# Scores and slot reads in the h banks, two tiled groups a batch, and later x loads

## The chip, the cores and the metric

The kernel runs on one core of a Trainium2 chip. The metric is the time of one execution on the device, in microseconds (us), as the median of several runs; profiles are one execution each. "Span" is the time from the first to the last instruction of the profiled execution. Every run has a state: fast, or slow when it is more than 1.5% above the fastest run of the same kernel. Ratios below use fast runs alone; a median is over all runs of a kernel.

## The reference, cut to what matters

```python
def _attn_ref(x, state):              # x (8, 8, 512, 64), state (8, 8, 32, 64)
    scores = scale * np.matmul(x, state.transpose(0, 1, 3, 2))
    a = softmax(scores)               # each token over the 32 slots
    xread = np.matmul(a, state)
    scores2 = scale * np.matmul(state, x.transpose(0, 1, 3, 2))
    a2 = softmax(scores2)             # each slot over the 512 tokens
    sread = np.matmul(a2, x)
    return np.concatenate([xread, sread], axis=2)

def _moe_ref(x, w_in, w_out, s, b):   # x (4352, 512), w_in (512, 2048)
    r = np.maximum(x @ w_in, 0.0)
    return (s * (r * r) + b) @ w_out
```

The softmaxes are abbreviated here. Both read the same scores, once along the slots and once along the tokens.

## The kernel before

The kernel first builds M = state x w_in for a batch, so that `a @ M` gives the hidden layer directly. It loops over batches s = 1 to 7. While it computes the products of batch s it prepares batch s+1: scores T, their exponential E, its transpose ET, the normalized shares, four chunks of M, and the slot reads V. I call one turn of this loop a **stage**. A stage has 16 "h pairs", f = 0 to 15, and the products of the second layer are spread between them as 112 products of 256 columns each. Each h pair goes through relu on ACT (`r`) and a square on DVE (`g`). The second layer is made of seven block products instead of eight, the **fast products**: they read sums of token blocks (`s`) and differences of weight blocks (`wd`), add up in oA, oB and oC, and DVE keeps the partial results `qa`, `qb` and `u`. For a batch below NDT the denominators of the shares come from products (D). From NDT on DVE makes them from ET, and a transfer brings the shares back as a4; I call this the **transposed softmax**.

Four buffers and queues matter to the argument. The first is how the PSUM banks are shared out: two "att" tiles for the preparation, two "h" banks for the hidden layer, and two for the output.

```python
    psA = ctx.enter_context(tc.tile_pool(name="psA", bufs=2, space=bass.MemoryType.PSUM))
    psH = ctx.enter_context(tc.tile_pool(name="psH", bufs=2, space=bass.MemoryType.PSUM))
    psO = ctx.enter_context(tc.tile_pool(name="psO", bufs=2, space=bass.MemoryType.PSUM))
```

The second is the SP queue. Every transposing transfer is issued there, in program order: xT (x transposed, which T multiplies), ET, a4 (the shares transposed back), the slot reads (srT) and stT (the state of batches 3 to 7 transposed).

```python
    def att_xT_dma(b):
        xT = new_xT(b)
        nc.sync.dma_start_transpose(
            out=xT.rearrange("p h k t -> p (h k) t"),
            in_=xn[b].rearrange("p h c d -> p (h c d)"),
        )
    ...
    def att_a4_dma(b):
        a = A[b]
        a["a4"] = apool.tile([P, NG, S], FP16, name=f"a4_{b}", tag="a4")
        nc.sync.dma_start_transpose(
            out=a["a4"].rearrange("p g (c t) -> p (g c) t", c=SCH),
            in_=a["aT"].rearrange("t j p -> t (j p)"),
        )
```

The third is the POOL queue, which issues the x loads and the output stores. The fourth is DVE, which makes the shares, the squares of relu, the sums of token blocks (`s`) that the fast products read, and the outputs (`osb`).

```python
            nc.vector.reduce_sum(den, ET_s, axis=mybir.AxisListType.X)
            with nc.allow_low_precision("shares are fp16"):
                nc.vector.reciprocal(inv, den)
            nc.vector.tensor_mul(...)            # aT = ET x inv, cut
```

The schedule of a stage says after which pair f a piece stands in the program. It sets the order in each queue; it does not set a time. This is the list of before for s of 2 and more, with its last lines cut:

```python
            if s + 3 < B:
                at(13 if s == 2 else 2, lambda: load_x(s + 3))
            if s == 2:
                at(0, stT_dma)
            if nb < B:
                at(3, lambda: att_T(nb, [0, 1]))
                at(3, lambda: att_M(nb, 0, "act"))
                at(4, lambda: att_ET(nb))
                if s in (2, 3):
                    at(4, lambda: att_xT_dma(nb + 1))
                if s >= 3 and s + 3 < B:
                    at(13, lambda: att_xT_dma(s + 3))
                if nb < NDT:
                    at(5, lambda: att_D(nb, [0, 1]))
                else:
                    at(8, lambda: att_shares(nb))
                    at(9, lambda: att_a4_dma(nb))
                at(7, lambda: att_M(nb, 1, "act"))
                at(7, lambda: att_M(nb, 2, "act"))
```

The softmax here doesn't subtract the row's maximum and nothing guards it: scores larger than these inputs give would overflow.

## Time and profile before

| | before |
|---|---|
| time, median of the first 3 runs | 211.18 us (211.03 to 213.14) |
| span of the profile | 208.0 us |
| last product of PE starts | 204.09 us |
| start of stage s=1, its length | 26.99, 25.27 us |
| stages s=2 to s=6 | 23.24, 21.27, 21.27, 21.28, 21.27 us |
| from the start of s=7 to the end | 47.41 us |

Stage lengths run from the first h product of a batch to the first one of the next. The prediction below shows the views on which it rests. The list of issues on the SP queue has the columns start, time on the queue, engine, line, operation, tiles and count.

### The profile page before, as it was taken

What the parts mean: (1) busy time and instruction counts of PE and PEld (TensorE: products, weight loads), DVE (VectorE), ACT (ScalarE), POOL (GpSimd) and SP (SyncE); (2) the same over time, 40 slices, a digit from 0 to 9 for tenths busy, and PEclk for the clock granted to TensorE, in tenths of its full rate; (3) what the DMA queues carried; (4) which work ended last, traced back from release to release, by engine and by line L of the source; (5) the groups of instructions that cost most, each with busy time, mean ns of one, the idle gap of its engine ahead of it and who ended that gap; (6) DMA issues with size and microseconds to landing.
All of it is one profiled execution on the core that took longest, in us unless ns stands there. A gap on an engine that the chain in (4) does not pass through costs nothing.

```text
span 208.0 us, 4757 instructions
## 1 busy us (share of the span) xinstructions
PE 199.5 (96%) x1947; PEld 129.4 (62%) x1947; DVE 162.1 (78%) x282; ACT 125.3 (60%) x218; POOL 37.6 (18%) x64
## 2 busy tenths in 40 slices
PE   7888999999899999999999999999999999999992
PEld 2433343445566676667666766676667777788882
DVE  1587825978769796899779977998799877895862
ACT  3678865698489557765776477656774544533100
POOL 5970001501110330123011201120111012100210
PEclk9999999999999999999999999999999999999999
DMA  5999996999947299979833915231324111110143
GB/s 183 225 202 206 207 191 104 179 181 174 266 52 153 72 194 123 124 163 185 127 103 67 196 52 102 54 107 54 101 29 132 50 54 50 54 50 0 54 145 111
DMA packets 45946, 25.35 MB, mean 122 GB/s; under 512 B 30884, under 2 KB 43940, under 8 KB 45924
## 3 DMA queue, kind: packets, MB, share of 16 engines
q0 software_dynamic: 15536, 16.19, 38.8%
q1 hardware_dynamic: 29588, 8.49, 23.8%
q10 hardware_dynamic: 800, 0.36, 0.7%
q8 instruction: 15, 0.25, 0.5%
q14 instruction: 7, 0.06, 0.1%
HBM read 17.33 MB, written 8.91 MB: 126 GB/s over the span
## 4 chain that ended last, share of the span: by engine, by line
PE 82%; DVE 6%; DMA 6%; ACT 4%; issue 1%; POOL 0%; SPq 0%; POOLq 0%
PE h L70 23%; PE oB L70 17%; PE oC L70 12%; PE oA L70 10%; PE o L70 6%; PE Mps L70 4%; DMA wi<-in_moe_w_in_dram 4%; PE h_sr L70 3%; DMA stT_all<-st 2%; ACT r L365 2%; DVE g L371 1%; PE T L70 1%; PE oB_sr L70 1%; PE V L70 1%; DVE M L298 1%; PE oA_sr L70 1%
## 5 line engine op out<-in xcount | busy, mean ns | idle before, releaser
L365 ACT ACTIVATE r<-h 128x512 f16<-128x512 f32 x126 | 74.4, 601 | 52.0 <-PE h L70 51.4
L70 PE MATMUL h<-a,M 128*128 128x512 f16 x256 | 75.0, 379 | 0.9 <-DVE M L298 0.6
L371 DVE TENSOR_TENSOR g<-r 128x1024 f16<-128x1024 f16 x64 | 44.1, 691 | 16.0 <-ACT r L365 15.8
L70 PEld LDWEIGHTS <-s 128*128 128x128 f16 x448 | 42.8, 98 | 19.3 <-issue 3.7
L70 PEld LDWEIGHTS <-g 128*128 128x128 f16 x400 | 38.0, 98 | 18.9 <-issue 2.9
L536 POOL DMA_DIRECT2D out_dram<-osb x27 | 18.2, 675 | 125.5 <-DVE osb L528 120.3
L70 PE MATMUL oB<-wd,s 128*128 128x256 f16 x224 | 32.7, 273 | 0.0
L70 PE MATMUL oA<-wo,g 128*128 128x256 f16 x224 | 31.6, 273 | 0.1
L70 PEld LDWEIGHTS <-M 128*128 128x128 f16 x256 | 24.6, 98 | 10.9 <-DVE M L298 1.6
L301 ACT CAST M<-Mps 128x1024 f16<-128x1024 f32 x27 | 26.8, 1017 | 1.4 <-PE Mps L70 0.8
L70 PE MATMUL oC<-wd,s 128*128 128x256 f16 x112 | 16.5, 273 | 0.0
L70 PE MATMUL o<-wo,g 128*128 128x512 f16 x64 | 16.3, 380 | 0.0
L70 PE MATMUL oB<-wd,g 128*128 128x256 f16 x112 | 15.9, 273 | 0.0
L70 PE MATMUL oC<-wo,s 128*128 128x256 f16 x112 | 15.3, 273 | 0.0
L365 ACT ACTIVATE r_sr<-h_sr 128x256 f16<-128x256 f32 x16 | 6.1, 382 | 8.4 <-PE h_sr L70 8.4
L227 ACT ACTIVATE E<-T 128x512 f16<-128x512 f32 x16 | 9.4, 596 | 1.2 <-PE T L70 1.1
L471 DVE TENSOR_TENSOR s<-s,g 128x1024 f16<-128x1024 f16 x14 | 9.7, 691 | 0.4
L70 PE MATMUL h_sr<-srdT,wi 128*128 128x256 f16 x64 | 9.6, 273 | 0.0
L465 DVE TENSOR_TENSOR s<-g 128x1024 f16<-128x1024 f16 x14 | 9.6, 685 | 0.0
L473 DVE TENSOR_TENSOR s<-g,s 128x1024 f16<-128x1024 f16 x14 | 9.6, 684 | 0.0
L469 DVE TENSOR_TENSOR s<-g,g 128x1024 f16<-128x1024 f16 x14 | 9.6, 683 | 0.0
L528 DVE SCALAR_TENSOR_TENSOR osb<-oC,s_bc,u 128x512 f32<-128x512 f32 x12 | 8.9, 746 | 0.5 <-PE oC L70 0.5
(102 smaller groups left out, 187.4 us busy)
## 6 DMA issues: line engine op xcount, KB each, us to landing
out_dram<-osb POOLq DMA_DIRECT2D x31, 256.0 KB, 2.8
xn<-in_x_dram POOLq DMA_DIRECT2D x7, 512.0 KB, 7.0
wi<-in_moe_w_in_dram POOLq DMA_DIRECT2D x4, 512.0 KB, 9.2
wo<-in_moe_w_out_dram POOLq DMA_DIRECT2D x4, 512.0 KB, 15.9
xf<-in_x_dram SPq DMA_DIRECT2D x2, 512.0 KB, 4.8
out_dram<-osb_sr SPq DMA_DIRECT2D x8, 32.0 KB, 1.6
out_dram<-osb_sr ACTq DMA_DIRECT2D x8, 32.0 KB, 1.7
out_dram<-osb_last SPq DMA_DIRECT2D x2, 128.0 KB, 1.9
```

The costliest lines, as they stand in the source:

```text
L70: return nc.tensor.matmul(out, lhsT, rhs, start=start, stop=stop, tile_position=tp, is_transpose=is_transpose, skip_group_check=True,)
L227: nc.scalar.activation(a["E"][:, g, :].rearrange("p (m t) -> p m t", m=2), T[:, :, 256 * i : 256 * i + 256], AF.Exp, scale=scale, accum_ou ...
L298: nc.vector.tensor_copy(dst[:, 0], two[0])
L301: nc.scalar.copy(dst, ps)
L365: nc.scalar.activation(r16[:, f % 2], hps, AF.Relu)
L371: nc.vector.tensor_mul(gt[:, f % 4 - 1 : f % 4 + 1], r16, r16)
L465: nc.vector.tensor_sub(o, a11, a21)
L469: nc.vector.tensor_add(o, a21, a22)
L471: nc.vector.tensor_sub(o, SQ[b, 1, j], a11)
L473: nc.vector.tensor_sub(o, a12, SQ[b, 2, j])
L528: nc.vector.scalar_tensor_tensor(osb, acc[bank], s_bc, add, ALU.mult, ALU.add)
L536: nc.gpsimd.dma_start(dst[j][:, :, n0 : n0 + NH], osb)
```

## The change

Its intent is to take overhead off PE, which bounds the kernel (it holds 82% of the chain of before): two groups of tiled products instead of three in a batch, scores and slot reads in the h banks so that the att tiles are free for M, and no D products for batch 3. The slot-read scaling goes from DVE to ACT. The x loads move later, and xT of the next batch moves behind a4. The diff, cut to its core:

```diff
-    NDT = 4
+    NDT = 3
...
+        one_bank = b >= NDT
+        if one_bank:
+            Ts = [psH.tile([P, NG, S // 2], FP32, tag="h", name=f"T_{b}_{m}") for m in range(2)]
...
+        if one_bank:
+            for m in range(2):
+                for g in gs:
+                    nc.scalar.activation(
+                        a["E"][:, g, 256 * m : 256 * m + 256],
+                        Ts[m][:, g, :],
+                        AF.Exp,
...
+        if b >= NDT - 1:
+            ps = psH.tile([P, NG, D], FP32, tag="h", name=f"V_{b}")
...
-        for g in range(NG):
-            nc.vector.tensor_scalar(a["sr"][:, g], ps[:, g], a["rq"][:, g : g + 1], None, ALU.mult)
+        with tc.issue_after(G["relu"]):
+            for g in range(NG):
+                nc.scalar.mul(a["sr"][:, g], ps[:, g], a["rq"][:, g : g + 1])
...
+                at(7, stT_dma)                                   # in stage s=1
...
-                at(13 if s == 2 else 2, lambda: load_x(s + 3))
-            if s == 2:
-                at(0, stT_dma)
+                at(13 if s == 2 else 12, lambda: load_x(s + 3))
             if nb < B:
-                at(3, lambda: att_T(nb, [0, 1]))
-                at(3, lambda: att_M(nb, 0, "act"))
+                ahead(4, lambda: att_M(nb, 0, "later"))
+                ahead(4, lambda: att_T(nb, [0, 1]))
+                ahead(4, lambda: att_M(nb, 1, "later"))
                 at(4, lambda: att_ET(nb))
-                if s in (2, 3):
-                    at(4, lambda: att_xT_dma(nb + 1))
-                if s >= 3 and s + 3 < B:
-                    at(13, lambda: att_xT_dma(s + 3))
...
+                at(4, lambda: A[nb]["M", 0]())
+                at(6, lambda: A[nb]["M", 1]())
+                at(8, lambda: att_shares(nb))
+                at(9, lambda: att_a4_dma(nb))
+                if nb + 1 < B:
+                    at(9, lambda: att_xT_dma(nb + 1))
...
+            ahead(10, lambda: att_V(s))
+            if nb < B:
+                ahead(10, lambda: att_M(nb, 2, "later"))
+                ahead(10, lambda: att_M(nb, 3, "later"))
+                at(10, lambda: A[nb]["M", 2]())
+                at(12, lambda: A[nb]["M", 3]())
...
+                if s > 1 and 4 <= f < 13:
+                    for fn in items[f]:
+                        fn()
+                    items[f] = []
```

More of the change, by code (lines that the diff above doesn't have):

```diff
@@ L210, in att_T @@
         a = A[b]
-        n = len(gs)
-        T = att_ps([P, 2, 512], FP32, f"T_{b}_{gs[0]}")
+        one_bank = b >= NDT
+        if one_bank:
+            Ts = [psH.tile([P, NG, S // 2], FP32, tag="h", name=f"T_{b}_{m}") for m in range(2)]
+        else:
+            T = att_ps([P, 2, 512], FP32, f"T_{b}_{gs[0]}")
+            Ts = [T[:, m, 0 : 256 * len(gs)].rearrange("p (g t) -> p g t", t=256) for m in range(2)]
         for q in range(NQ):
@@ L217, in att_T @@
                     mm(
-                        T[32 * q : 32 * q + 32, m, 256 * i : 256 * i + 256],
+                        Ts[m][32 * q : 32 * q + 32, i, :],
                         st_of(b, h, m),
@@ L224, in att_T @@
             a["E"] = apool.tile([P, NG, S], FP16, name=f"E_{b}", tag="E", bufs=3)
-            a["rs"] = apool.tile([P, NG], FP32, name=f"rs_{b}", tag="rs", bufs=4)
+            n = 2 * NG if one_bank else NG
+            a["rs"] = apool.tile([P, n], FP32, name=f"rs_{b}", tag="rs", bufs=4)
+        if one_bank:
[5 more added lines that the diff above has]
+                        AF.Exp,
+                        scale=scale,
+                        accum_out=a["rs"][:, NG * m + g : NG * m + g + 1],
+                    )
+            return
         for i, g in enumerate(gs):
@@ L277, in att_a4_dma, with copy_M @@
         )
+    def copy_M(dst, ps):
+        with tc.issue_after(G["relu"]):
+            nc.scalar.copy(dst, ps)
     def att_M(b, c, how):
@@ L296, in att_M @@
         dst = a["M"][:, :, FC * c : FC * c + FC]
-        if how == "split":
+        if how == "later":
+            a["M", c] = lambda: copy_M(dst, ps)
+        elif how == "split":
             nc.vector.tensor_copy(dst[:, 0], two[0])
@@ L309, in att_ET @@
         a["rq"] = apool.tile([P, NG], FP32, name=f"rq_{b}", tag="rq", bufs=4)
-        nc.vector.reciprocal(a["rq"], a["rs"])
+        rs = a["rs"]
+        if b >= NDT:
+            rs = apool.tile([P, NG], FP32, name=f"rt_{b}", tag="rt")
+            nc.vector.tensor_add(rs, a["rs"][:, 0:NG], a["rs"][:, NG : 2 * NG])
+        nc.vector.reciprocal(a["rq"], rs)
     def att_V(b):
         a = A[b]
-        ps = att_ps([P, NG, D], FP32, f"V_{b}")
+        if b >= NDT - 1:
+            ps = psH.tile([P, NG, D], FP32, tag="h", name=f"V_{b}")
+        else:
+            ps = att_ps([P, NG, D], FP32, f"V_{b}")
         for g in range(NG):
@@ L326, in att_V @@
         a["sr"] = apool.tile([P, NG, D], FP16, name=f"sr_{b}", tag="sr")
-        for g in range(NG):
-            nc.vector.tensor_scalar(a["sr"][:, g], ps[:, g], a["rq"][:, g : g + 1], None, ALU.mult)
+        with tc.issue_after(G["relu"]):
+            for g in range(NG):
+                nc.scalar.mul(a["sr"][:, g], ps[:, g], a["rq"][:, g : g + 1])
     def att_srT_dma(b):
@@ L365, in mm1_close @@
             nc.scalar.activation(r16[:, f % 2], hps, AF.Relu)
+            G["relu"] = nc.cur_bb.bb.instructions[-1]
         if f % 4 == 0:
@@ L756, in at, with ahead @@
                 out.setdefault(f, []).append(fn)
+            def ahead(f, fn):
+                out.setdefault((f, "ahead"), []).append(fn)
             if s == 1:
@@ L780, in pieces @@
             if s + 3 < B:
-                at(13 if s == 2 else 2, lambda: load_x(s + 3))
-            if s == 2:
-                at(0, stT_dma)
+                at(13 if s == 2 else 12, lambda: load_x(s + 3))
             if nb < B:
-                at(3, lambda: att_T(nb, [0, 1]))
-                at(3, lambda: att_M(nb, 0, "act"))
+                ahead(4, lambda: att_M(nb, 0, "later"))
+                ahead(4, lambda: att_T(nb, [0, 1]))
+                ahead(4, lambda: att_M(nb, 1, "later"))
                 at(4, lambda: att_ET(nb))
-                if s in (2, 3):
-                    at(4, lambda: att_xT_dma(nb + 1))
-                if s >= 3 and s + 3 < B:
-                    at(13, lambda: att_xT_dma(s + 3))
-                if nb < NDT:
-                    at(5, lambda: att_D(nb, [0, 1]))
-                else:
-                    at(8, lambda: att_shares(nb))
-                    at(9, lambda: att_a4_dma(nb))
-                at(7, lambda: att_M(nb, 1, "act"))
-                at(7, lambda: att_M(nb, 2, "act"))
+                at(4, lambda: A[nb]["M", 0]())
[4 more added lines that the diff above has]
+                    at(9, lambda: att_xT_dma(nb + 1))
             if s == 2:
@@ L802, in pieces @@
                 at(12, lambda: att_srT_dma(1))
-            at(10, lambda: att_V(s))
+            ahead(10, lambda: att_V(s))
[4 more added lines that the diff above has]
+                at(12, lambda: A[nb]["M", 3]())
             if s == last_b:
@@ L807, in pieces @@
                 at(12, lambda: att_srT_dma(s))
-            if nb < B:
-                at(10, lambda: att_M(nb, 3, "act"))
             if s == last_b:
@@ L832 @@
             for f in range(NKF):
+                for fn in todo_s.get((f, "ahead"), []):
+                    fn()
+                if s > 1 and 4 <= f < 13:
+                    for fn in items[f]:
+                        fn()
+                    items[f] = []
                 mm1_x(s, f)
```

## The prediction

> **What bounds the kernel now.** I read the page first (engine shares, chain of waits), then the stretches view cut at batch boundaries, then the PE, ACT, DVE and SP timelines. The chain:
>
> ```profile
> PE 199.5 (96%) x1947; PEld 129.4 (62%) x1947; DVE 162.1 (78%) x282; ACT 125.3 (60%) x218; POOL 37.6 (18%) x64
> ...
> PE 82%; DVE 6%; DMA 6%; ACT 4%; issue 1%; POOL 0%; SPq 0%; POOLq 0%
> ```
>
> The set-up and batch 0 hold most of the chain's DMA and DVE part; from about 58 us on it is PE. The loop over batches s = 1..7 computes s's products while it prepares batch s+1. I place its stage starts at the 16 h pairs (two 512-column products each):
>
> ```profile
> 52.26:75.50 23.24, 22.42 (x261) 14.89 (x259) 18.66 (x33) 16.06 (x26) 3.50 (x5) 1.00 0.64 136
> 75.50:96.77 21.27, 21.27 (x227) 14.58 (x224) 18.68 (x31) 14.17 (x25) 3.61 (x5) 1.00 1.03 154
> 96.77:118.05 21.28, 21.28 (x227) 14.59 (x225) 18.68 (x31) 14.18 (x25) 3.60 (x5) 1.00 0.65 127
> ```
>
> After the window come its length, then PE, PEld, DVE, ACT and POOL busy. Stages s=3 to s=6 each take 21.27 us with PE full; s=2 takes 23.24. Clock is 1.00, so a gain must take work or gaps off PE. PE's timeline in s=3, start time first:
>
> ```profile
> 84.55 0.59 PE L70 MATMUL h<-a,M 128*128 128x512 f16 x2
> 85.08 0.63 PE L70 MATMUL Mps<-wi,stT_all 64*32 64x512 f16 x16
> 85.64 0.94 PE L70 MATMUL oC<-wd,s 128*128 128x256 f16 x7
> 86.41 0.59 PE L70 MATMUL h<-a,M 128*128 128x512 f16 x2
> 86.84 0.93 PE L70 MATMUL oC<-wd,s 128*128 128x256 f16 x7
> ...
> 88.80 0.59 PE L70 MATMUL h<-a,M 128*128 128x512 f16 x2
> 89.33 0.42 PE L70 MATMUL V<-xn,ET 128*32 128x64 f16 x32
> 89.67 0.41 PE L70 MATMUL Mps<-wi,stT_all 64*32 64x512 f16 x8
> 90.02 0.94 PE L70 MATMUL oB<-wd,g 128*128 128x256 f16 x7
> ```
>
> Starts, not durations, are to be read. An h pair costs 0.43 (86.41 to 86.84), seven 256-column products 0.77. Before a tiled group the pair takes 0.53, so **entry costs 0.10**. Sixteen Mps take 0.56; eight of them cost 0.213 (T, also eightfold parallel, takes 0.23 ahead of Mps in one mode), so 0.43 is work and **exit costs 0.13**. V to Mps changes the mode again, 0.34 for about 0.21 of work. A stage has three groups: T+M0 (after pair 3), M1+M2 (after 7), V+M3 (after 10). Overhead is 3 x 0.23 + 0.13 = 0.82. Check: 112 x 0.109 + 16 x 0.43 + four M x 0.213 + T 0.21 + V 0.21 + 0.82 = 21.2, against 21.27.
>
> Stage s=2's excess of 1.97 us:
>
> ```profile
> 54.67 0.59 PE L70 MATMUL h<-a,M 128*128 128x512 f16 x2
> 55.29 0.94 PE L70 MATMUL oB<-wd,s 128*128 128x256 f16 x7
> 56.06 0.59 PE L70 MATMUL h<-a,M 128*128 128x512 f16 x2
> 57.45 0.43 PE L70 MATMUL T<-xT,stT_all 64*32 64x256 f16 x16 [0.79 <-DMA stT_all<-st]
> ```
>
> T starts 1.39 after its pair instead of 0.53: 0.86 lost to the stT transpose, which the SP timeline shows issued at 52.83 and the transfers view landing 4.6 us later. The oB products start 0.62 after their pair, 0.19 late; the waits view names DVE's token sum. The rest is D of batch 3 (two products, 0.43) and a second V in a group of its own (0.10 + 0.35): 0.86 + 0.19 + 0.43 + 0.45 = 1.93.
>
> [...]
>
> **The change part by part.**
>
> *Two groups instead of three* (M0+T+M1 before pair 4, V+M2+M3 before pair 10), s=2 to s=6: one entry and one exit fewer, 0.23 each.
>
> *h banks.* T takes both. ACT's timeline in s=2, where nothing queues before it:
>
> ```profile
> 57.98 0.60 ACT L227 ACTIVATE E<-T 128x512 f16<-128x512 f32 x1 [0.69 <-PE T L70]
> 58.48 0.19 ACT L227 ACTIVATION_READ_ACCUMULATOR E<-T 128x1 f32 x1
> 58.57 0.59 ACT L227 ACTIVATE E<-T 128x512 f16<-128x512 f32 x1
> ```
>
> T starts at 57.45, M at 57.68, call that t; Exp starts at t+0.30 and the pitch is 0.59. With 256 columns it is 0.59 - 0.21 = 0.38. The first bank's two Exps and the last accumulator read end near t+0.30+0.38+0.48 = 1.16, plus 0.06 to reach PE (an assumption) = 1.22. On PE there now lie M1 0.21, exit 0.13 and seven products 0.77 before pair 4: t+1.11. So a stall of at most 0.11; I count half. The second bank is free at about t+1.9, pair 5 due at 2.3: no wait. V's bank: V finishes about 1.07 after pair 9's start, relu 9 ends at 1.23, [...]and its next user comes at about 3.4: none. Net 0.17 per stage, 5 x 0.17 = **-0.85**.
>
> *ACT* gains four Exp passes for two (4 x 0.38 - 2 x 0.59 = +0.34)[...], off the path. M0's copy (1.02) after relu 4 delays relu 5 by some 0.3, while its bank is not wanted for 1 us.
>
> *Slot reads off DVE:* -0.47 per batch, on DVE alone. For V of batch 0 (DVE at 50.91, in a stretch 99% busy) it lets the sums come 0.4 earlier, which should remove the 0.19 stall: **-0.19**.
>
> *Transposed softmax for batch 3:* D's two products go, **-0.43**; ACT loses 1.02 + 1.06. DVE gains 1.21 + 0.35 + 1.23 and loses the 0.69 multiply and two scaling pairs (0.94): +1.2 on 18.7 in a stage of some 21.5. The shares have about 8 us until their use: hidden.
>
> *stT transpose in stage s=1:* SP is free at 39.5, the state copy on POOL was done at 33.0; it lands near 44. T of batch 3 then waits only for its xT, issued at 46.2, which lands near 52 to 54: **-0.86**.
>
> *Late x loads:* no PE wait names them; 0.
>
> *Order.* Fast products now come before pairs 4 to 12, after from 13, so pairs 12 and 13 adjoin. In s=7 slot products lie between: h12, h_sr, h13. h13 needs h12's bank, whose relu ends 1.23 after h12's start (85.18 + 0.60 against 84.55); h13 is due at 0.87: **+0.4**. In other stages pair 13 needs pair 11's bank, long free.
>
> Sum: -0.85 - 0.19 - 0.43 - 0.86 + 0.4 = -1.93, so 211.18 - 1.93 = 209.25, say **209.2 us**.
>
> **Rivals.** *The lent banks starve PE.* If ACT runs an M copy before the Exps, or relu 3 is late, pair 4 waits another 1.0 per batch: +5, about 214. For: only two h banks, and Tile orders ACT itself. Against: the copies are tied behind relu 4, and ACT idles 0.6 between relus. *The stT wait merely becomes an xT wait.* The earlier transpose shares DMA engines (share above 1.0 in s=1) with the x load on which xT 3 waits. If it slips over 3 us the 0.86 stays: 210.1. Against: T also moves one pair later. *DVE becomes the bound in s=2:* shares delay the squares, relu buffers fill, PE stops; a microsecond at most, about 210.2. For: DVE at 4.93 of 5 us in 85 to 90, where shares run now. Against: PE showed no gap there. *Larger gain:* no bank stall, no tail stall, tiled gaps smaller than thought: about -2.6, 208.6.
>
> **Range and chances.** The gain terms sum to -2.6 with no losses; the likely single failures add 0.5 to 1. Runs before spread by 1% (211.03 to 213.14). So 207.9 to 210.8. Faster by 2% needs 206.96, twice my gain: 0.05. Slower by 2% needs the starved banks: 0.03.
>
> **What will show it.** Right: two tiled groups per stage; stages s=3 to s=6 at 21.05 to 21.15; s=2 near 21.6 with T not waiting on stT; pair 4 no later than 1.22 after M1's start; a 0.4 gap before h13 in s=7. Wrong: PE rows waiting on E or relu each stage, stages above 21.3, or T waiting on xT.

The step that V's bank holds nothing up, and the one that ACT stays off the path, are estimates. In after the two scalings of batch 0 took 0.53 us together (at 50.49), and ACT was busy for 14.61 to 14.65 us in each of the stages s=3 to s=6.

Figures without a row beside them in that text have these in before. Products of 256 columns last 273 ns and start 0.11 us apart. Eight Mps take 0.22 us (43.11 to 43.33) and T 0.23 (57.45 to 57.68), so 0.213 and 0.21 are estimates, half of an h pair's 0.43. A change of "mode" is a change of the tile shape in the rows (128*128, 64*32, 128*32). An ACT pass takes 596 ns for 512 columns (Exp) and 382 for 256 (relu), which differ by the 0.21 that is subtracted for the pitch of the Exps. From the end of an accumulator read on ACT to the product that needs it PE took 0.05 us (21.49 to 21.54), where 0.06 is assumed. The DMA share of s=1 is 1.17.

## More of the kernel before

```profile
81.49 1.26 SPq L308 DMA_TRANSPOSE ET<-E  x1
82.84 3.83 SPq L204 DMA_TRANSPOSE xT<-xn  x1
90.04 1.23 SPq L274 DMA_TRANSPOSE a<-aT  x1
```

This is stage s=3, which starts at 75.50. The xT row is that of batch 5, and it is issued right behind ET of batch 4. Batch 5 needs it for T in stage s=4, which PE starts at 100.88. The transfer therefore has a **lead** of 18 us. Those of batches 6 and 7, issued at 92.94 and 114.21, have 29 us each (T at 122.16 and 143.43).

## The result, and the profile after

| | before | after |
|---|---|---|
| time, median of 4 fast runs | 211.11 us (210.02 to 213.14) | 223.28 us (223.22 to 224.07) |
| span, mean granted clock | 208.0 us, 1.000 | 221.4 us, 0.983 |
| start of s=1, its length | 26.99, 25.27 | 27.16, 25.25 |
| stages s=2, 3, 4, 5, 6 | 23.24, 21.27, 21.27, 21.28, 21.27 | 25.22, 22.90, 28.12, 22.45, 21.55 |
| from s=7 to the end | 47.41 | 48.75 |

The change makes the kernel slower: the ratio is 1.0573, with a 95% interval of 1.049 to 1.0657. A ratio here is always the mean time of one kernel's fast runs over that of the other's of the same rounds, so it is not quite the ratio of the medians quoted. The prediction of 209.2 us in a range of 207.9 to 210.8 missed.

Engine shares, granted clock and chain of waits, from the page of after:

```profile
PE 202.9 (92%) x1945; PEld 130.3 (59%) x1945; DVE 160.2 (72%) x273; ACT 126.9 (57%) x252; POOL 37.6 (17%) x64
...
PEclk9999999999999999999769999999999999999999
...
PE 50%; DMA 27%; DVE 13%; ACT 5%; issue 2%; SPq 1%; POOL 0%; POOLq 0%
DMA xT<-xn 21%; PE h L70 12%; PE oB L70 11%; PE oC L70 7%; DMA xn<-in_x_dram 5%; ACT r L395 3%; PE oA L70 3%; PE o L70 3%; DVE g L402 3%; PE Mps L70 3%; PE warm_ps L70 3%; PE h_sr L70 2%; DVE s L500 1%; PE T L70 1%; PE oB_sr L70 1%
```

PE's part of the chain fell from 82% to 50%. The transposed x, which was on no chain before, holds 21%. Clock is 1.00 but for two slices. The stretches view, cut at the stage starts (columns as in the prediction), shows where:

```profile
52.41:77.63 25.22, 22.27 (x259) 14.68 (x257) 19.63 (x33) 14.99 (x32) 4.18 (x6) 1.00 0.68 133
77.63:100.53 22.90, 21.72 (x227) 14.54 (x224) 18.61 (x31) 14.64 (x31) 3.60 (x5) 1.00 0.67 114
100.53:128.65 28.12, 23.07 (x224) 15.47 (x225) 17.53 (x30) 14.65 (x30) 3.61 (x5) 0.88 0.70 96
151.10:172.65 21.55, 21.43 (x226) 14.62 (x224) 18.18 (x31) 14.61 (x31) 2.71 (x4) 1.00 0.41 96
```

In s=3 to s=6 of before, PE was as busy as the stage was long, and in s=2 it was free for 0.82 us. Now 2.95 of 25.22 us are free in s=2, 1.18 in s=3 and 5.05 in s=4. In s=6, the last row, the gap is small, and still the stage is 0.28 longer than before. PE's timeline names the wait; the bracket at the end is the idle time ahead of the row and what ended it:

```profile
60.45 0.44 PE L70 MATMUL T<-xT,stT_all 64*32 64x256 f16 x16 [1.98 <-DMA xT<-xn]
83.98 0.44 PE L70 MATMUL T<-xT,stT_all 64*32 64x256 f16 x16 [0.72 <-DMA xT<-xn]
110.88 0.65 PE L70 MATMUL T<-xT,stT_all 64*32 64x256 f16 x16 [5.05 <-DMA xT<-xn]
113.36 1.06 PE L70 MATMUL h<-a,M 128*128 128x512 f16 x2
156.65 0.40 PE L70 MATMUL T<-xT,stT_all 64*32 64x256 f16 x16
```

The T of batches 3, 4 and 5 waited 1.98, 0.72 and 5.05 us; that of batch 6 waited another 0.71 (the waits view sums all four to 8.5 us), that of batch 7 none. The row at 113.36 is an h pair that takes 1.06 us where it took 0.59: the clock was lowered in the long wait. The granted clock was 0.62 from 107 to 111 us and 0.53 from 111 to 115, which in these last four loses 0.47 x 4 = 1.9 us; from 115 to 119 it was 1.00. The waits of 1.98 us and less left the clock at 1.00 in this trace, and the one of 5.05 us did not. Waits of other lengths are met below.

Four waits and the slow clock give 8.46 + 1.9 = 10.4 of the 13.4 us that the span grew. The other 3.0 are the subject of the later experiments. (Before had a wait of 0.79 at T itself, for stT; less that, the T waits and the clock account for 9.6.)

Why xT is late can be read from the SP and POOL queues of stage s=3 (start 77.63) and from the median times from issue to landing:

```profile
95.53 1.25 SPq L290 DMA_TRANSPOSE a<-aT  x1
96.87 4.89 SPq L204 DMA_TRANSPOSE xT<-xn  x1
96.99 1.01 POOL L120 DMA_DIRECT2D xn<-in_x_dram  x1
...
xn<-in_x_dram POOLq DMA_DIRECT2D x7, 512.0 KB, 11.7
xT<-xn SPq DMA_TRANSPOSE x6, 9.4
stT_all<-st SPq DMA_TRANSPOSE x1, 14.4
```

The same three transfers took 7.0, 5.8 and 4.6 us before. The xT of batch 5 now stands behind a4 and is issued at 96.87. PE would have started T at 110.88 - 5.05 = 105.83, so the lead is 9.0 us, where it was 18. And the transfer, which was now issued 0.12 us ahead of an x load (96.99 on the POOL queue), took 13.96 us by the chain. 13.96 - 8.96 is the wait of 5.0. The other batches fit the same sum:

| xT of batch | issued | x load issued after it by | xT took | lead to T | T waited |
|---|---|---|---|---|---|
| 4 | 74.00 | 0.78 | 9.94 | 9.26 | 0.72 |
| 5 | 96.87 | 0.12 | 13.96 | 8.96 | 5.05 |
| 6 | 125.52 | 1.08 | 9.53 | 8.86 | 0.71 |
| 7 | 147.97 | no load | not shown | 8.68 | none |

Here the lead is the time from issue to where T would have started without its wait. Moving xT cost it half of its lead, and the late x loads, put into the same part of the stage, made it take longer than what was left.

### The profile page after: what moved, and what is told of

Its sections match the earlier page's. It is cut to its first block, busy times and chain, and to the rows that moved or that the text cites. A ratio compares the mean times of both kernels' runs of the same rounds, so it can differ in the third digit from the quotient of the medians.

```text
span 221.4 us, 4780 instructions
## 1 busy us (share of the span) xinstructions
PE 202.9 (92%) x1945; PEld 130.3 (59%) x1945; DVE 160.2 (72%) x273; ACT 126.9 (57%) x252; POOL 37.6 (17%) x64
## 4 chain that ended last, share of the span: by engine, by line
PE 50%; DMA 27%; DVE 13%; ACT 5%; issue 2%; SPq 1%; POOL 0%; POOLq 0%
DMA xT<-xn 21%; PE h L70 12%; PE oB L70 11%; PE oC L70 7%; DMA xn<-in_x_dram 5%; ACT r L395 3%; PE oA L70 3%; PE o L70 3%; DVE g L402 3%; PE Mps L70 3%; PE warm_ps L70 3%; PE h_sr L70 2%; DVE s L500 1%; PE T L70 1%; PE oB_sr L70 1%
## 5 line engine op out<-in xcount | busy, mean ns | idle before, releaser
L395 ACT ACTIVATE r<-h 128x512 f16<-128x512 f32 x126 | 74.4, 602 | 51.1 <-PE h L70 46.1
L70 PEld LDWEIGHTS <-s 128*128 128x128 f16 x448 | 43.5, 99 | 20.6 <-DVE s L502 3.9
L70 PE MATMUL oB<-wd,s 128*128 128x256 f16 x224 | 33.3, 277 | 0.8 <-DVE s L502 0.4
L70 PEld LDWEIGHTS <-M 128*128 128x128 f16 x256 | 24.6, 98 | 13.3 <-DVE M L320 1.6
L297 ACT CAST M<-Mps 128x1024 f16<-128x1024 f32 x20 | 20.1, 1006 | 0.0
L70 PE MATMUL oB<-wd,g 128*128 128x256 f16 x112 | 15.9, 273 | 0.0
L234 ACT ACTIVATE E<-T 128x256 f16<-128x256 f32 x20 | 7.4, 384 | 13.5 <-PE T L70 13.5
L559 DVE SCALAR_TENSOR_TENSOR osb<-oA,s_bc,bias_bc 128x512 f32<-128x512 f32 x7 | 5.2, 749 | 13.3 <-PE oA L70 13.3
L70 PE MATMUL T<-xT,stT_all 64*32 64x256 f16 x80 | 2.4, 299 | 8.5 <-DMA xT<-xn 8.5
## 6 DMA issues: line engine op xcount, KB each, us to landing
xn<-in_x_dram POOLq DMA_DIRECT2D x7, 512.0 KB, 11.7
```

Source lines behind the costliest of these rows:

```text
L70: return nc.tensor.matmul(out, lhsT, rhs, start=start, stop=stop, tile_position=tp, is_transpose=is_transpose, skip_group_check=True,)
L234: nc.scalar.activation(a["E"][:, g, 256 * m : 256 * m + 256], Ts[m][:, g, :], AF.Exp, scale=scale, accum_out=a["rs"][:, NG * m + g : NG * ...
L297: nc.scalar.copy(dst, ps)
L395: nc.scalar.activation(r16[:, f % 2], hps, AF.Relu)
L559: nc.vector.scalar_tensor_tensor(osb, acc[bank], s_bc, add, ALU.mult, ALU.add)
```

## The experiments

Theory **A** is the one just told: the loss is in the transfers, from xT's place behind a4 together with the x load that runs beside it. Rival **B** is that of the prediction: the h banks lent to T and V starve PE, or more generally the changed compute is what costs. For what is left without the xT waits, two more were set against each other: **C**, the copies of M that now sit between the two relus of a pair and so delay DVE's squares and sums, and **D**, the new order of fast products and h pairs. Kernels of one call ran on the same chip beside the kernel before. Fifteen kernels ran, and all were correct.

| run | median us, all runs | before, same rounds | ratio, 95% |
|---|---|---|---|
| compute only | 212.30 | 210.53 | 1.0084 (1.005 to 1.0118) |
| transfers only | 212.00 | 210.53 | 1.0042 (0.9968 to 1.0117) |
| loads early | 214.82 | 210.53 | 1.0221 (1.0166 to 1.0276) |
| xT before a4 | 213.89 | 210.53 | 1.0139 (1.0076 to 1.0202) |
| after again | 220.70 | 210.41 | 1.0468 (1.0419 to 1.0517) |
| pairs first | 214.42 | 210.41 | 1.0175 (1.0132 to 1.0218) |
| copies odd | 211.91 | 210.41 | 1.0092 (1.0042 to 1.0141) |
| softmax and stT | 210.47 | 210.41 | 1.0010 (0.9972 to 1.0048) |
| gated load | 221.02 | 210.11 | 1.0417 (1.0359 to 1.0474) |
| stT late | 221.73 | 210.11 | 1.0549 (1.0533 to 1.0565) |
| odd only | 212.78 | 210.11 | 1.0125 (1.0085 to 1.0166) |
| combined | 211.40 | 210.11 | 1.0053 (1.003 to 1.0076) |
| squares on ACT | 209.65 | 210.27 | 0.9964 (0.9935 to 0.9994) |
| before, squares on ACT | 210.51 | 210.27 | 0.9995 (0.9958 to 1.0031) |
| softmax, squares on ACT | 210.45 | 210.27 | 1.0007 (0.9976 to 1.0038) |

The profiles of pairs first and of gated load are of slow executions; from these two I read landing times, single waits and, for gated load, the clock and the stages of this one execution.

### The two halves by themselves

**Compute only** is the changed kernel with the transfers of before:

```diff
-                at(7, stT_dma)                                   # s=1
...
-                at(13 if s == 2 else 12, lambda: load_x(s + 3))
+                at(13 if s == 2 else 2, lambda: load_x(s + 3))
+            if s == 2:
+                at(0, stT_dma)
...
-                if nb + 1 < B:
-                    at(9, lambda: att_xT_dma(nb + 1))
+                if s in (2, 3):
+                    at(4, lambda: att_xT_dma(nb + 1))
+                if s >= 3 and s + 3 < B:
+                    at(13, lambda: att_xT_dma(s + 3))
```

> The changed kernel with all three transfer moves undone (x loads, xT transposes and the stT transpose where the kernel before had them); the PE, ACT and softmax part of the change stays. Theory A (the loss is transfers: the xT transposes now share the DMA engines with the x loads and come too late for T): the waits of T on xT in stages s=2 to s=5 vanish, leaving stages s=3 to s=6 at about 21.5 us, as s=6 is in the changed kernel, where T waits for nothing; the whole at 210 to 213 us, near the kernel before. Rival B (lending h banks to T and V, and ACT's longer chain, cost most of it): stays above 218 us with PE waiting on E or relu.

**Transfers only** is the kernel before with the same lines the other way round: the places of xT, x loads and stT from the changed kernel, and nothing else of it.

> The kernel before with only the three transfer moves of the change (x loads after pair 12, xT after pair 9, stT in stage s=1). If the transfer moves alone make the loss (A): 219 to 224 us. If they need the later shares of the changed kernel, because xT stands behind a4 in the SP queue and a4 waits for DVE (A2: in the kernel before a4 is issued 14.5 us after its stage's start, in the changed one 17.9): the collision in s=3 to s=5 mostly does not happen, only the stT and x collision before s=2 stays, 212 to 214 us. Rival B: about 211.

Compute only took 212.30 us, transfers only 212.00. Neither is near the 220 to 223 us of both together. So the loss is neither in the compute nor in the transfers alone. It is an **interaction**, and rival B falls as its cause (what the compute costs alone is 0.8%, with an interval above 1): with everything lent and regrouped, the stages are 22.27, 21.83, 21.51, 22.09 and 21.55, and the waits view has no wait for a transposing xT.

What the two halves do to each other can be read from where things are issued in stage s=3. With transfers only, a4 goes out 14.5 us after the stage's start, as before, and xT behind it at 15.9; the x load follows 2.0 us after xT. That xT took 9.76 us and T waited 0.22. The next one, 2.9 us ahead of its load, took 7.01, and T did not wait. With both halves, a4 goes out at 17.9, because the last step of DVE's shares starts later (16.6 after the stage's start instead of 13.3), and xT at 19.2. So xT moved by 3.4 us. The x load moved by 1.5 (17.9 to 19.4), and the two now start 0.12 us apart.

### xT and a4 exchanged, and early loads

**xT before a4** changes the order of two neighbours in the SP queue and nothing else:

```diff
                 at(8, lambda: att_shares(nb))
-                at(9, lambda: att_a4_dma(nb))
                 if nb + 1 < B:
                     at(9, lambda: att_xT_dma(nb + 1))
+                at(9, lambda: att_a4_dma(nb))
```

> The changed kernel with one swap: xT is issued before a4 in the SP queue, both still after pair 9. A2 (xT is held up behind a4, which waits for DVE's shares, and is so pushed into the x load): xT goes some 5 us earlier, lands before or soon after the load starts, T's waits in s=3 to s=5 vanish and stages fall to about 21.6: about 214 to 216 us, s=2 unchanged at 25. If the place in the queue is not what matters: stays at 221 to 224. B: no change.

**Loads early** leaves xT behind a4 and puts the x loads back:

```diff
-                at(13 if s == 2 else 12, lambda: load_x(s + 3))
+                at(13 if s == 2 else 2, lambda: load_x(s + 3))
```

> The changed kernel with only the x loads put back (after pair 2 from s=3 on). A: the xT transposes of s=3 and s=4 run alone and take 4.5 to 6 us in place of 14.0 and 9.5, so T's waits in s=4 and s=5 (5.05 and 0.71 us, and the clock drop after the first) vanish; those in s=2 and s=3 stay, since the x load of s=2 keeps its place: 223.3 less about 7.5 is 215.8. B: no change, 223.

**After again** is the changed kernel once more, on the chip of three later runs, to see that its loss repeats.

> The changed kernel again, unaltered, on the chip of the next three runs, because the runs that shared its code up to the middle of stage s=2 showed x of batch 3 landing at 48.4 to 48.9 us where its own profile had 51.05. If the loss is a property of the kernel: 221 to 224 us. If part of it hangs on how the transfers happen to fall on a chip: 217 to 221, with T's waits on xT in the same stages but shorter ones.

The exchange of two lines brought 213.89 us, a ratio of 1.0139 where after has 1.0573 and, again, 1.0468. In s=3 its xT was issued well ahead of a4, and landed in 5.70 us with no load beside it:

```profile
83.88 4.09 SPq L204 DMA_TRANSPOSE xT<-xn  x1
91.95 1.23 SPq L290 DMA_TRANSPOSE a<-aT  x1
```

The waits view has no wait for a transposing xT. The first h pair of s=4 waited 0.70 us for a4. This is not the price of the exchange: a4 went out 16.98 us after the stage's start, just as in compute only, where the same pair waited 0.23, and after waited 0.38 there.

The early loads brought 1.0221: T of batches 4 and 6 still waited 0.37 and 0.31 (xT of batch 4 took 9.59 us with a load beside it), and the 5 us wait was gone, though an x load still began 2.6 us after the xT of batch 5. After again had the long wait of 5.00 us once more; its xT of batch 5 began 0.12 us ahead of the load, and the chain gives it 13.83 us. So the long wait goes when either of the two conditions of theory A is changed, xT's place behind a4 or the moment of the x load.

Not all that the two runs gained is due to their edits. Their code is that of after up to the middle of s=2, and I had expected their s=2 to stay at 25 us, but both have 22.27, mainly because T of batch 3 did not wait in these executions. The edits are to be judged by s=3 to s=5: 73.47 us in sum in after and 73.08 in after again, 65.72 with xT before a4, 66.61 with the loads early, 63.82 in before.

Why a queue position matters so much can be read from the SP queue of after in s=3. The data of the xT had landed long before (x of batch 5 at 85.05 at the latest), and the queue issued nothing from the end of ET's row at 87.37 to 95.53. Then a4 went out, 0.07 us after DVE had ended the last step of the shares (95.46), and xT 1.34 us after a4. In all four stages of after that have such a pair, s=2 to s=5, it is 1.33 or 1.34 us, and xT never went out before the a4 ahead of it.

### The load held back until xT is in

**Gated load** keeps the two apart by data instead of by order. A one-element copy on POOL reads the new xT, and the x load stands behind it:

```diff
+            def gated_x():
+                nc.gpsimd.tensor_copy(gate, A[nb + 1]["xT"][0:1, 0, 0, 0:1])
+                load_x(s + 3)
...
-                at(13 if s == 2 else 12, lambda: load_x(s + 3))
+                at(13 if s == 2 else 12, gated_x)
```

> The changed kernel with the x loads of s=2 to s=4 held on POOL until the xT transpose issued before them has landed (a one-element copy that reads xT, then the load); nothing else moves. Theory A (two transfers in flight together stretch each other): xT takes 5 to 6.5 us in place of 9.1 to 14.0, T's waits in s=3 to s=5 vanish, stages near 22.3, 21.7, 21.7: 212 to 214 us. If xT is slow by itself when issued so late, or T waits for something else: 219 to 221. Output stores stand behind the held load on POOL, which may give back up to 1 us.

The mechanism held: xT of batches 4 and 6 took 5.81 and 7.59 us where it had 9.94 and 9.53, the gate read that of batch 5 by 5.4 us after its issue, where it had taken 13.96, the x loads took 6.21 to 6.65, and no T of s=3 to s=5 waited. The total did not follow: 221.02 us, and 217.91 and 219.94 in the two fast runs. I had expected far less to be given back. The waits view of the profiled, slow execution:

```profile
PE T L70 <- DMA xT<-xn: 2.9, 1, 2.9
PE oC L70 <- DVE osb L559: 2.2, 2, 1.6
PE oA L70 <- DVE qa L585: 1.6, 3, 0.6
```

The first row is batch 3, whose xT is not ordered against a gated load. After this wait of 2.91 us the stretches view gives a clock of 0.50 from 62 to 66 us, and stage s=2 is 28.90 us long. This is the largest part of this execution's loss, 5.7 of 12.6 us against before, and the gate has no part in it. Stages s=3 to s=5 sum to 68.42 us, against 73.47 in after and 65.72 with xT before a4. So the gate gained there, and new waits took part of it back. The output stores go through the same POOL queue, so they stood behind the held load; POOL's timeline has a store at 77.84, then nothing until the gate's copy at 83.60, a wait of 5.09 us. That the oC and oA waits come from output buffers which these stores free late is my reading of it; no run separated it from the other things DVE does then. Why the two fast runs stay near 218 to 220 us has no profile.

### The stT transpose

**stT late** puts it back to the start of s=2 in the changed kernel:

```diff
-                at(7, stT_dma)
...
+            if s == 2:
+                at(0, stT_dma)
```

> The changed kernel with only the stT transpose put back to the start of stage s=2. The early stT shares the engines with the x loads of batches 3 and 4 (landing after 11 to 14 us in place of 4.6) and makes x and xT of batch 3 late: without it stage s=2 falls from 24.1 to 25.2 to about 22.3, the rest stays: 218 to 219 us. The prediction's own step (early stT is worth 0.86) would make this kernel slower, 221.5 or more.

It took 221.73 us, between after and after again: no gain or loss that can be told, and my expectation of a gain missed. PE's timeline at M0, the first of the group, where T had waited for xT in after:

```profile
58.52 0.41 PE L70 MATMUL Mps<-wi,stT_all 64*32 64x512 f16 x8 [1.29 <-DMA stT_all<-st]
```

So one wait took the place of the other. The transfers of stage s=1 tell why. In the nine profiles with stT at f=7 of s=1 it is issued near 39.8, between the x loads of batches 3 and 4, and lands only after 10.8 to 14.8 us. The x load of batch 3, which xT of batch 3 needs, then takes 8.9 to 11.7 us, against 7.0 to 9.8 in the eight other profiles, and xT is issued at 48.4 to 51.1 instead of 46.2 to 49.1. The ranges overlap: in stT late the load took 9.8 and in combined 8.9, with no stT beside it, so its length is not set by stT alone. What it costs also changes from execution to execution. With the same code up to there, T of batch 3 waited 1.6 to 2.9 us for xT in after, after again, pairs first, copies odd and gated load, and not at all in loads early, xT before a4 and odd only. Transfers only shows the exchange most purely: its T of batch 3 waited 1.13 us on xT, where before waited 0.79 on stT, and its s=2 is 23.58 instead of 23.24.

**Softmax and stT** is the kernel before with batch 3 by transposed softmax and with stT at f=10 of s=1, behind the xT of batch 3:

```diff
-    NDT = 4
+    NDT = 3
...
                 at(10, lambda: att_T(2, [0, 1]))
+                at(10, stT_dma)
...
-            if s == 2:
-                at(0, stT_dma)
```

> The kernel before with only two of the parts: the transposed softmax also for batch 3, and the stT transpose issued between xT of batch 3 and ET of batch 2, so that it neither meets the x load of batch 3 nor comes after ET. By the prediction's own steps these are worth 0.43 + 0.86 in stage s=2: stage s=2 at 21.9 in place of 23.24, others unchanged at 21.27, 209.5 to 210 us where the kernel before has 210.5 to 211. If DVE, with 2.1 us more in s=2, is the bound there: s=2 stays above 22.5.

Here stT is issued at 50.99, lands in 3.79 us, and T of batch 3 waits for nothing. Stage s=2 is 22.49, and PE's last product starts at 203.40 instead of 204.09. So this part of the change is worth 0.7 us on PE in this profile, when it stands in the right place of the queue. It did not reach the time (ratio 1.001): the end of the span came 4.5 us after that product's start, where before has 3.9, and the runs spread by more than the gain. Of the 1.3 us that the two parts promise, 0.55 goes to a new wait of oC for DVE's `osb` in s=2.

### What is left: copies or order

With xT before a4, stages s=3, s=5 and s=6 are still 22.31, 22.01 and 21.55 us. PE's timeline of that run at the start of s=6:

```profile
142.32 0.27 PE L70 MATMUL oB<-wd,s 128*128 128x256 f16 x1
142.62 0.82 PE L70 MATMUL oA<-wo,g 128*128 128x256 f16 x6
143.28 0.59 PE L70 MATMUL h<-a,M 128*128 128x512 f16 x2
143.95 0.94 PE L70 MATMUL oB<-wd,s 128*128 128x256 f16 x7
```

One oB product takes 0.11 from start to start, and here 0.30; an h pair takes 0.43, and here 0.67. These are 0.19 and 0.24 us in which PE waited, in the first for DVE's `qa`, in the second for the token sum. Before has neither. That DVE is late by the stage's end and carries it over is tested below.

**Pairs first** tests D on top of the last kernel: fast products again stand behind the pairs, except beside the groups.

```diff
-                if s > 1 and 4 <= f < 13:
+                if s > 1 and f in ((10,) if s == last_b else (4, 10)):
```

> xT before a4, and besides the fast products come after their h pair again, but for pairs 4 and 10 (which need the time for the lent banks); in the last stage only for pair 10. Theory D (what is left of the loss, about 3 us, is DVE: with products first, pairs 4 and 5 come 1.5 us later in the stage, DVE starves there for 1.6 us, and then, saturated, is late with the token sums and qa at the next stage's start, where PE waits 0.2 + 0.24 us; and pair 13 waits 0.4 in the last stage): those waits vanish, against a new wait of pair 5 on T's second bank of up to 0.3: stages s=3 to s=6 at 21.1 to 21.4, the tail after s=7's start 47.9 in place of 48.8, 211 to 212 us in place of 213.9. Rival C (the M copies between the two relus of a pair are what delays DVE): no change beyond the tail, 213.

**Copies odd** adds C to that, **odd only** has C without D:

```diff
-                at(4, lambda: A[nb]["M", 0]())
-                at(6, lambda: A[nb]["M", 1]())
+                at(5, lambda: A[nb]["M", 0]())
+                at(7, lambda: A[nb]["M", 1]())
...
-                at(10, lambda: A[nb]["M", 2]())
-                at(12, lambda: A[nb]["M", 3]())
+                at(11, lambda: A[nb]["M", 2]())
+                at(13, lambda: A[nb]["M", 3]())
```

> As the run before, and the four M copies moved behind the second relu of their pair (after pairs 5, 7, 11, 13). C: squares come up to 0.9 us earlier on DVE, stages fall by 0.3 or more each against the run before, 1.5 us in all or more. D: within 0.5 us of the run before.

> xT before a4, and only the four M copies moved behind the second relu of their pair (the order of products and pairs as in the changed kernel). C (the copies between the two relus hold up the squares, so DVE is late for the next stage's sums): the waits of 0.20 and 0.24 us at each stage's start vanish without the 0.30 that pair 5 waited when pairs came first: stages s=3 to s=6 at 21.0 to 21.2, about 1.5 to 2.5 us below the run with xT before a4 (213.9), so 211.5 to 212.4. If D were needed too: stages stay at 21.5.

Pairs first took 214.42 us and kept both waits (0.20 and 0.25 in s=6), with a third of 0.30 at pair 5: D by itself falls. Odd only has s=6 at 21.34 instead of 21.55, and the `qa` wait of that stage is gone while the sum's (0.23) stays. In s=5 the `qa` wait stays too, and the stage with it (22.02). With D added, s=6 is 21.40. So C carries 1.1 us over the stages s=2 to s=6 of these profiles, 0.2 a stage, and D nothing that can be seen there. In time odd only is at 1.0125 and copies odd at 1.0092, with overlapping intervals, so the time separates neither of them from xT before a4.

**Combined** is odd only with stT at f=10 of s=1, and with the order of before in s=7:

```diff
-                at(7, stT_dma)
...
                 at(10, lambda: att_T(2, [0, 1]))
+                at(10, stT_dma)
...
-                if s > 1 and 4 <= f < 13:
+                if s > 1 and (4 <= f < 13 if s < last_b else f == 10):
```

> All that the runs point to in one kernel: xT before a4, M copies after the second relu, stT issued between xT of batch 3 and ET of batch 2, products first only before pair 10 in the last stage. Stages s=2 at 21.8, s=3 to s=6 at 21.1, the tail after s=7's start 48.0: 0.23 x 4 + 1.4 - 0.6 = 1.7 us below the kernel before, about 209. If DVE or the transfers still bind somewhere, 210 to 211.

It took 211.40 us, a ratio of 1.0053: still a little slower than before. From the start of s=7 to PE's end it has 44.0 us where odd only has 44.4. That is the 0.4 us of the pairs 12 and 13, which this order does not make adjoin.

### Less work on DVE

What is left should then be DVE's lateness. **Squares on ACT** takes two of eight squares a batch off DVE, on top of combined:

```diff
         if f % 2 == 1:
-            nc.vector.tensor_mul(gt[:, f % 4 - 1 : f % 4 + 1], r16, r16)
-            G["last"] = nc.cur_bb.bb.instructions[-1]
+            if key != "sr" and key >= 2 and f in (1, 15):
+                nc.scalar.activation(gt[:, f % 4 - 1 : f % 4 + 1], r16, AF.Square)
+            else:
+                nc.vector.tensor_mul(gt[:, f % 4 - 1 : f % 4 + 1], r16, r16)
+                G["last"] = nc.cur_bb.bb.instructions[-1]
```

> The combined run, and from stage s=2 on two of its eight squares (pairs 14+15 and 0+1) are made by ACT, which idles there, in place of DVE: 1.2 us of DVE work less in the stretch where DVE has no idle time. If DVE's lateness is what is left of the loss (in the combined run PE waits about 2.7 us in stages s=2 to s=7 on qa, the sums and what stands behind them): those waits shrink to a quarter, stages s=3 to s=6 at 21.05 to 21.15, 209 us or a little less, below the kernel before (210.1 to 210.5). If the lateness is not DVE's load but comes with the order of the pairs (inputs arriving late whatever DVE's load): stages stay at 21.3 to 22.0, 211.4.

**Before, squares on ACT** is the control: the same edit on the kernel before. **Softmax, squares on ACT** has it on softmax and stT.

> Control: the kernel before with the same two squares on ACT. Its PE waits for DVE for only 0.2 us in s=2, so no more than 0.3 us is to be gained: 210 to 210.5. If it gains 1 us or more, the gain of the other run is not about the change.

> Transposed softmax for batch 3 and stT ahead of ET on the kernel before (which gained nothing: s=2 fell by 0.75, of which 0.55 went to a new wait of PE for DVE), with the two squares on ACT. If that wait is DVE's load: it goes, s=2 at 21.95 in place of 22.49, 209.5 to 210.

Squares on ACT took 209.65 us against 210.27 of before in the same rounds: a ratio of 0.9964 with an interval just below one. It is a third of a percent faster than before, far less than the 2% from which the record calls a kernel faster. Its stages are 22.06, 21.28, 21.42, 21.40 and 21.10, and PE's last product starts 1.1 us earlier than before. The same place at the start of s=6 as above:

```profile
140.20 0.27 PE L70 MATMUL oB<-wd,s 128*128 128x256 f16 x1
140.31 0.82 PE L70 MATMUL oA<-wo,g 128*128 128x256 f16 x6
140.97 0.59 PE L70 MATMUL h<-a,M 128*128 128x512 f16 x2
141.40 0.93 PE L70 MATMUL oB<-wd,s 128*128 128x256 f16 x7
```

Both waits are gone: 0.11 and 0.43 from start to start. The control stayed at 0.9995, so within its interval the squares gain nothing by themselves. (In its profile the end after s=7's start is 0.2 us shorter on PE, and s=2 is 0.36 longer, where T waited 1.16 us for stT.) So DVE's load was the larger part of what was left. It is not all mended, and I had expected the waits to shrink to a quarter: one wait of 0.50 in s=2 (the token sum) and others of 0.18, 0.23 and 0.24 us are left in the loop. On softmax and stT the edit gained nothing either, and the oC wait in s=2 stayed (0.56), so that wait is not due to those squares. What it is due to is open.

## Why the prediction was right or wrong

- **The step that failed** reads "*Late x loads:* no PE wait names them; 0." I looked at whether PE waited for the loads in the kernel before, and not at what the new places would do. There were two omissions. The diff moves xT behind a4 in the SP queue, where it goes out 1.33 to 1.34 us after a4 and never before it, and the prediction does not mention this move at all; it cut the lead from 18 to 29 us down to 9. And the load of x was put beside that xT, where both take longer: 13.96 us for the xT of batch 5 and 14.1 for the load beside it in after, against 8.3 and 6.3 for that xT and the load of the same stage in before. In place of 0 the runs showed 6.5 us of T waits (batches 4 to 6) and 1.9 us of slow clock. The two reversals, xT before a4 and loads early, show it in s=3 to s=5: 7.8 and 6.9 us less.
- **stT, -0.86: fell.** The rival "The stT wait merely becomes an xT wait" was right in kind and sized too small. It named the shared transfers with "share above 1.0 in s=1" (1.17 in before), and asked for a slip of over 3 us. In after, xT of batch 3 was issued 4.9 us later than before, and T waited 1.98. Two terms were mis-sized: stT, "lands near 44", landed at 54.4, after 14.4 us, and xT of batch 3, "lands near 52 to 54", at 60.4. Where T did not wait (loads early, xT before a4), s=2 is 22.27, but compute only, with stT in its old place, has 22.27 as well, so the early stT brought nothing there either. Behind xT of batch 3 it landed in 3.79 to 5.5 us and cost no wait.
- **The lent banks starve PE: right to reject.** Pair 4's wait was at most 0.11 by the prediction, and 0.08 in the s=6 of xT before a4. The pitch of the Exp passes came out as 0.35 to 0.38 in after, 0.36 in the mean, where I had taken 0.38.
- **Groups and h banks, -0.85: right in mechanism, not in the sum.** There are two groups a stage, with an entry of 0.10. But s=6 came out at 21.55, not at 21.05 to 21.15: DVE's waits of 0.19 and 0.24 were not in the sum. With DVE relieved, the same stage is 21.10, inside the range I had given.
- **M copies.** I wrote that M0's copy delays relu 5 while its bank is not wanted, and looked only at the bank. The result of that relu is also awaited by DVE's square, and moving the copies brought 0.21 in s=6.
- **Slot reads off DVE, -0.19: right, but not in the profile of after.** The oB product of s=2 follows its pair after 0.43 in nine of the twelve profiles with the slot reads on ACT, and after 0.62 in all five with them on DVE. In after it stayed at 0.62 (55.38 to 56.00), with a new oB wait of 0.40 at the stage's start. There DVE itself had waited 0.85 us at 52.0, for an output store to land and free its `osb`; so it was in gated load.
- **Transposed softmax for batch 3, -0.43, and rival "DVE becomes the bound in s=2".** The D products are gone, and DVE's busy time in s=2 rose from 18.66 to 19.63. In compute only s=2 is 22.27, with a new oC wait of 0.70 for the token sum; without it, it would be the 21.6 that I had given. In softmax and stT the new wait for DVE is 0.55. Both have the size that this rival was given ("a microsecond at most").
- **Order in s=7, +0.4: right.** The gap before h13 is 0.41, and undoing it in combined gave 0.4 back.
- **Chances.** Slower by over 2% had 0.03, tied to one way of failing. I gave nothing to a transfer that becomes late, though the change moves three of them.

## What to carry to other kernels

Work out for each transfer that is moved what stands before it in its own queue, when that one's data are ready, and so what lead is left to its first reader; then add what is issued in the same moment on the other queues. Here a lead of 18 us would have hidden every xT that was seen (13.96 us at most), and one of 9 us did not, as soon as a neighbour made the transfer take 10. Where an engine is nearly full, as DVE here (4.93 of 5 us from 85 to 90 in before), a rearrangement that adds no work to it can still cost through what delays its inputs: here 0.21 us in s=6, which moving the copies of M gave back.

## What the traces showed of transfers, tiles, ACT and the clock

- From stage s=2 on, xT took 5.7, 8.3 and 5.8 us in before (batches 4, 5 and 7), where no x load was issued in the 2 us after it, and 9.94, 13.96 and 9.53 us in after (batches 4, 5 and 6), where one was. From stage s=1 on, the x load of 512 KB took 5.9 to 7.0 us in four of five cases of before (10.5 in the fifth), and 9.1 to 14.6 in after.
- In after an xT whose data were there went out 1.34 us after a4, which waited for DVE, and exchanging the two took 7.8 us off the stages s=3 to s=5 (73.47 us to 65.72).
- In before a group of tiled products cost 0.10 us on entry (84.55 to 85.08, where a pair otherwise takes 0.43) and 0.13 on exit (85.08 to 85.64, of which 0.43 is work by the prediction's estimate).
- On ACT the relu of 512 columns took 602 ns in the mean in after, the Exp of 256 columns 376 to 393 ns, and the scaling of 64 columns 308 to 328 ns.
- The clock was 0.50 from 62 to 66 us after a wait of 2.91 us in gated load (a slow execution; the shortest such wait in a fast profile is 3.71 us, in stT late, with 0.50 from 108 to 112), and stayed at 1.00 after one of 1.98 us in after. What lies between was not measured.
